# A scheduled attention and Hyena kernel: the order of work behind the first batch laid anew

## The chip, the cores and the metric

One core of one Trainium2 chip runs the whole program. The metric is device time in microseconds (us); the times shown are medians of several runs. A profile is one execution with the hardware profiler on. The engines are PE (matmuls; PEld is its weight load), ACT (activations and copies), DVE (vector work), POOL (casts, and issue of some DMAs) and SP (issues most DMAs).

## The reference

Softmax attention with one added to the denominator (8 batches, 12 heads, 448 positions, 64 wide) gives x, 448 x 768 for a batch. A Hyena-like layer follows: x is projected to three parts, the second is convolved along the sequence with a given filter by FFT, the three are multiplied, and the product is projected again.

```python
attn = e / (np.sum(e, axis=-1, keepdims=True) + np.exp(-m) + 1e-09)
x = np.matmul(attn, v)                # then heads side by side: (B, 448, 768)
proj = x @ w_proj                     # 768 -> 3 * 768
x1, x2, x3 = proj[..., :D], proj[..., D:2*D], proj[..., 2*D:]
X2 = np.fft.rfft(x2, n=S, axis=1)
H = np.fft.rfft(filter_fft, n=S, axis=0)[None, :, :]
y = x1 * np.fft.irfft(X2 * H, n=S, axis=1) * x3
out = y @ w_out
```

## The kernel before

Everything is bf16 on PE with f32 sums in PSUM's eight banks. The work is cut into 2,137 tasks, each some instructions of one engine: `attention(i)` makes them for each of 48 pairs of heads (scores L871 and L873, exponentials L884 and L890 on ACT, products with v L902 and L910, division L923 to L925 on DVE), `staged(b)` and `loaded(b)` make the loads of q, k and v on SP and their casts on POOL, and `dense(b)` makes, for each batch, the folding (L1055, L1060), the second part's projection (L1083 or L1105), the short transforms (L1154, L1158, back L1253), the gates (L1206, L1222) and the last projection (L1019), copied out by ACT (L1332) and stored by SP (L1339, L1342).

A `Plan` collects the tasks. `add` gives each the next number of the table `plan.ORDER`; `run` then lets each engine take its tasks strictly by that number, and a model of the engines and DMAs decides which PSUM bank each task gets. `plan.TIMES` holds durations and lateness of DMAs for that model. The model also says where PE would stand idle between 4.6 and 44 us; `fillers` puts matmuls of zeros there (`fill`, L1501), each 128 columns, as many as fit in nine tenths of the modelled gap. Every engine runs its own queue in order; between engines there are semaphores.

The softmax is computed without taking the maximum off. `watch()` checks that this was safe: the smallest denominator is reduced on DVE (`judge`, L1417, L1418), a one-column matmul counts the bad rows (L1424), and DVE casts the count to the integer `flag` (L1426). Behind all planned tasks each engine loads `flag` into a register (L1559) and branches on it (L1561): if it isn't zero, everything is computed again in a safe form; with this input the branch is jumped over. The last projections of the last batch (five groups of six matmuls, with eight copies and six stores) are kept back and run behind that branch by `plan.rest()`. A hint ahead of the plan names the branch for PE and DVE alone.

```python
add("DVE", 0.35, tau(NHP * n_batches, 4.0), judge, need=[("low", b) for b in range(n_batches)], make=["bad"])
add("PE", 0.1, tau(NHP * n_batches, 4.0), lambda: nc.tensor.matmul(bank(hy)[0:1, 0:1], bad, one), need=["bad"],
    make=["count bad"], take=[hy])
add("DVE", 0.1, tau(NHP * n_batches, 4.0), lambda: nc.vector.tensor_copy(flag, bank(hy)[0:1, 0:1]), need=["count bad"],
    make=["flag"], give=[hy])
...
tc.mark_branch_hint_location("overflow", 0, engines=[E.PE, E.DVE])
plan.run()
...
overflow = nc.values_load(flag[0:1, 0:1], min_val=0, max_val=128)
with (
    tc.If(overflow > 0, label="overflow"),
```

Of the kernel before, what the change touches and what calls it, by code (L numbers as in the profile page):

```python
# [317 lines left out]
def kernel(  # L318
# [104 lines left out]
    def stage(g, at, n):  # L423
# [4 lines left out]
    plan = Plan(  # L428
        {
            "e": 6, "er": 2, "e3": 3, "er3": 1, "k0": 2, "q0": 2, "u": 1, "w": 1, "xf": 1,  # L430
            "x2": 1, "x2s": 1, "x2b": 2, "xs": 2, "t0": 2, "t1": 2, "yh": 1, "g": 1, "x1": 2, "cr": 2, "cw": 1, "cv": 2, "yT": 1, "yR": 1,
            "os": 3,
        }
    )
# [1125 lines left out]
    with (  # L1560
# [6 lines left out]
        for b in range(n_batches):  # L1567
            W["yT", b], W["yR", b // 2] = y, yr
            stable(b)
            plan = Plan(plan.size)  # L1570
# [9 lines left out]
    with tc.manual_schedule(engines={E.PE, E.Pool, E.DVE, E.Activation, E.SP}):  # L1580
        plan = main
# [31 lines left out]
```

## Time and profile before

| what | us |
|---|---|
| median of 3 runs | 369.39 |
| lowest and highest run | 368.69, 369.54 |
| the profiled execution's own time | 367.79 |
| its span, first to last instruction | 366.0 |

The profile's page lists the busy time of each engine, the costliest groups of instructions by source line, and the DMA queues. Other views of the same trace list waits (who waited for whom), the instructions in order of time with runs of like ones merged, all instructions of one line, and the chain of work that ended last. The DMA queue of the loads is at work 72.5% of the span, and 43.86 MB are read from HBM. In a view, "PEldq", "ACTq" or "SPq" is an engine's sequencer, which loads registers, branches and issues DMAs.

### The profile page before, as it was taken

How to read it: one execution, taken by the hardware profiler on the slowest of the kernel's cores; microseconds unless marked ns; L12 is line 12 of the kernel's file. 1: busy time of each engine (PE TensorE's matmuls, PEld its weight loads, DVE VectorE, ACT ScalarE, POOL GpSimd, SP SyncE). 2: the span in 40 equal slices, each digit the busy share in tenths (PEclk: the TensorE clock that was granted, in tenths of full speed). 3: DMA queues.
4: the chain of work that ended last, by engine and by line, in shares of the span. 5: the costliest groups of instructions: out<-in, count | busy, mean ns of one | idle time of the engine just before them, and what ended most of it. 6: DMA issues, size and time to landing. Idle time of an engine off the chain costs nothing. (4 is left out here: it accounts for less than half of the span.)

```text
span 366.0 us, 9373 instructions
## 1 busy us (share of the span) xinstructions
PE 359.8 (98%) x3625; PEld 216.4 (59%) x3625; DVE 259.1 (71%) x672; ACT 264.0 (72%) x454; POOL 115.9 (32%) x247
## 2 busy tenths in 40 slices
PE   8999999999999999999999999999999999999995
PEld 7666676666664766555465555655555556555553
DVE  5669398975889667574887667694478857758670
ACT  6998778777778688767678566778877884464443
POOL 8773482253443463413516343521110000000000
PEclk9999999999999999999999999999999999999999
DMA  8999999998999969899999999864964155044035
GB/s 215 279 246 245 238 180 228 246 190 199 193 256 281 214 204 217 226 226 183 264 226 240 270 211 238 246 162 108 204 119 130 45 88 131 0 88 131 1 134 175
DMA packets 132163, 68.41 MB, mean 187 GB/s; under 512 B 88781, under 2 KB 128528, under 8 KB 132112
## 3 DMA queue, kind: packets, MB, share of 16 engines
q1 hardware_dynamic: 127392, 62.11, 72.5%
q0 software_dynamic: 4480, 5.41, 8.6%
q8 instruction: 29, 0.48, 0.6%
q10 hardware_dynamic: 240, 0.23, 0.3%
q14 instruction: 22, 0.18, 0.1%
HBM read 43.86 MB, written 11.01 MB: 150 GB/s over the span
## 5 line engine op out<-in xcount | busy, mean ns | idle before, releaser
L884 ACT ACTIVATE e<-psum 128x896 bf16<-128x896 f32 x138 | 121.9, 920 | 25.6 <-PE psum L871 22.5
L1206 PE MATMUL psum<-xT,wproj_bf 128*128 128x448 bf16 x576 | 121.9, 353 | 0.0
L1206 PEld LDWEIGHTS <-wproj_bf 128*128 128x128 bf16 x576 | 54.2, 98 | 48.1 <-issue 3.9
L1019 PE MATMUL psum<-wout_bf,yT 128*128 128x384 bf16 (+2 forms) x288 | 54.9, 326 | 0.1
L910 PE MATMUL psum<-vn,e 128*128 128x65 bf16 x1104 | 44.8, 194 | 0.0
L910 PEld LDWEIGHTS <-e 128*128 128x128 bf16 x1104 | 39.4, 98 | 7.5 <-issue 3.6
L871 PE MATMUL psum<-qT,kT 64*128 64x448 bf16 x288 | 42.8, 354 | 0.1
L668 POOL CAST nat<-nat 112x512 bf16<-112x512 f32 x36 | 24.9, 695 | 53.4 <-DMA nat<-in_q_dram 53.3
L1332 ACT COPY osb<-psum 128x384 f32<-128x384 f32 (+2 forms) x56 | 26.0, 482 | 20.3 <-PE psum L1019 15.4
L1172 DVE TENSOR_TENSOR t<-xs,hrs 112x768 bf16<-112x768 bf16 (+1 forms) x64 | 36.5, 589 | 3.8 <-ACT xs L1166 3.4
L1019 PEld LDWEIGHTS <-yT 128*128 128x128 bf16 x288 | 26.7, 98 | 18.3 <-issue 1.4
L1105 PE MATMUL psum<-xf,wproj_bf 128*128 128x456 bf16 x180 | 37.5, 356 | 0.0
L1166 ACT CAST xs<-psum 112x384 bf16<-112x384 f32 (+1 forms) x64 | 28.9, 487 | 11.8 <-PE psum L1154 9.2
L1222 DVE TENSOR_TENSOR g<-x,psum 128x448 bf16<-128x448 bf16 x42 | 25.8, 617 | 14.2 <-PE psum L1206 9.6
L925 DVE TENSOR_TENSOR xb<-psum,den 128x512 bf16<-128x512 f32 x48 | 33.2, 691 | 1.6
L700 POOL CAST vn<-nat 128x192 bf16<-128x192 f32 x58 | 22.6, 421 | 33.5 <-DMA nat<-in_v_dram 33.4
L1220 ACT CAST x<-psum 128x448 bf16<-128x448 f32 x42 | 22.2, 538 | 13.7 <-PE psum L1206 13.4
L1262 ACT CAST cr<-psum 128x452 bf16<-128x452 f32 x48 | 24.1, 543 | 8.4 <-PE psum L1253 8.2
L890 ACT ACTIVATE er<-psum 128x448 bf16<-128x448 f32 x46 | 25.3, 553 | 6.5 <-PE psum L873 5.3
L688 POOL CAST nat<-nat 128x384 bf16<-128x384 f32 x29 | 17.0, 587 | 33.3 <-DMA nat<-in_k_dram 25.1
L923 DVE TENSOR_SCALAR den<-psum 128x8 f32<-128x8 f32 x48 | 7.8, 163 | 27.7 <-PE psum L910 19.7
L1105 PEld LDWEIGHTS <-wproj_bf 128*128 128x128 bf16 x180 | 16.8, 98 | 16.7 <-issue 1.9
(138 smaller groups left out, 499.9 us busy)
## 6 DMA issues: line engine op xcount, KB each, us to landing
nat<-in_q_dram SPq DMA_DIRECT2D x47, 224.0 KB, 4.4
out_dram<-osb SPq DMA_DIRECT2D x23, 384.0 KB, 3.6
nat<-in_k_dram SPq DMA_DIRECT2D x41, 192.0 KB, 4.1
nat<-in_v_dram SPq DMA_DIRECT2D x41, 192.0 KB, 4.7
wproj_bf<-in_moe_w_proj_dram POOLq DMA_DIRECT2D x2, 1152.0 KB, 12.1
rests<-in_k_dram SPq DMA_DIRECT2D x8, 192.0 KB, 5.2
rests<-in_v_dram SPq DMA_DIRECT2D x8, 192.0 KB, 4.2
out_dram<-osb SPq DMA_DIRECT2D x8, 192.0 KB, 2.9
```

The source lines that it names most:

```text
L871: nc.tensor.matmul(sc[:, u, 0:S], kT[b % 2][c, hp, t, :], qT[b % 2][c, hp, :])
L884: nc.scalar.activation(to, of, AF.Exp, scale=SCALE)
L890: nc.scalar.activation(to, of, AF.Exp, scale=SCALE)
L910: nc.tensor.matmul(out_bank(u)[:, n, :], P["e"][1 + t][:, u * S + n * 128 : u * S + n * 128 + 128], vn[b % 2][:, hp, 4 * u + t, :], start= ...
L925: nc.vector.tensor_tensor(W["xb", b][:, hp].rearrange("p n (u d) -> p u n d", u=2), op[:, :, :, 0:DH], rec[:].unsqueeze(3).to_broadcast([1 ...
L1019: nc.tensor.matmul(ops[:n, : c.stop - c.start], y[:, dt, 0:n], wout_bf[:, dt, c], start=(dt == 0), stop=(dt == NDT - 1),)
L1105: nc.tensor.matmul(pps, wproj_bf[:, kt, D + dt * 128 : D + (dt + 1) * 128], W["xf", b][:, kt], start=(kt == 0), stop=(kt == NDT - 1),)
L1166: nc.scalar.copy(L["xs", par, ch][:K, pg % 2, :], L["Z", pg, ch][:K, :DCH])
L1172: nc.vector.tensor_tensor(t[:K], L["xs", par, ch][:K], h, op=ALU.mult)
L1206: nc.tensor.matmul(p[:, :S], wproj_bf[:, kt, 2 * part * D + dt * 128 : 2 * part * D + (dt + 1) * 128], xT()[:, kt, 0:S], start=(kt == 0), ...
L1222: nc.vector.tensor_tensor(g[:, dt, :], L["x1", dt], p[:, :S], op=ALU.mult)
L1332: (nc.vector.tensor_copy if half else nc.scalar.copy)(L["os", st][:n, c.start + lo : c.start + hi], L["O", st, ch][:n, lo:hi])
```

## The change

Two tables of numbers are replaced, and nothing else. `plan.ORDER` has 2,137 numbers as before, of which 1,484 differ. `plan.TIMES` has other values of DMA lateness for 56 early loads (mostly some tenths of a microsecond more). Both lines are cut here to the start of the first table, its last four numbers, and one changed entry of the second.

```diff
-    plan.ORDER = (3, 0, 1, 159, 1, 2, 0, 0, 1,
...
-    4, 488, 666, 498)
-    plan.TIMES = {
...
-    36: (0.58, 0.735, 50.0, -0.6553),
...
+    plan.ORDER = (3, 0, 1, 166, 1, 2, 0, 0, 1,
...
+    4, 466, 707, 547)
+    plan.TIMES = {
...
+    36: (0.58, 0.735, 50.0, -0.0382),
...
```

The last three numbers of ORDER are those of `judge` on DVE, of the counting matmul on PE and of the flag's cast on DVE: in the change the matmul is PE's 708th task of 714 instead of its 667th, and the cast is DVE's 548th task of 549 instead of its 499th, the last one ahead of the branch.

On PE the first 138 tasks stand as before. Behind them 488 tasks have another place, by up to some forty places. The other queues are laid anew from about the same stage on: of DVE's 549 tasks 399 have another place, of ACT's 452 320, of SP's 244 172, of POOL's 178 105.

The flag on PE. The place in the last batch's short transforms where the counting product stood before (`ft` is the transform's table, `x_5282` the second part of the last batch, `bad` and `one` the check's operands):

```order
L1105 LDWEIGHTS wproj_bf
L1105 MATMUL psum<-xf,wproj_bf 128x456
L1154 LDWEIGHTS ft
L1154 MATMUL psum<-x_5282,ft 113x384
L1424 LDWEIGHTS bad
L1424 MATMUL psum<-one,bad 1x1
L1154 LDWEIGHTS ft
L1154 MATMUL psum<-x_5282,ft 113x384
L1206 LDWEIGHTS wproj_bf
L1206 MATMUL psum<-xT,wproj_bf 128x448
```

and the end of PE's planned work in the change (`yR` and `yT` are the gated product, `wout_bf` the last projection's weights):

```order
L1019 LDWEIGHTS yR
L1019 MATMUL psum<-wout_bf,yR 128x384
L1424 LDWEIGHTS bad
L1424 MATMUL psum<-one,bad 1x1
L1019 LDWEIGHTS yT
L1019 MATMUL psum<-wout_bf,yT 128x384
L1019 LDWEIGHTS yT
L1019 MATMUL psum<-wout_bf,yT 128x384
L1559 TENSOR_LOAD flag
L1561 COMPARE_AND_BRANCH
```

The product moved from amid the last batch to two matmuls ahead of the branch. In the change the end of DVE's planned work reads

```order
L1222 TENSOR_TENSOR g<-x_5651,psum 128x448
L1282 TENSOR_TENSOR cv<-cw 128x2x224
L1297 TENSOR_TENSOR yR<-g,cv 128x2x64
L1297 TENSOR_TENSOR yT<-g,cv 128x768
L1426 CAST flag<-psum 1x1
L1559 TENSOR_LOAD flag
L1561 COMPARE_AND_BRANCH
```

so that nothing stands between the cast of the flag and the loads of it. On SP the load of the flag stood ahead of three stores of the last planned rows,

```order
L1339 DMA out_dram<-osb 128x768 x2
L1559 TENSOR_LOAD flag
L1559 ISA x2
L1339 DMA out_dram<-osb 128x768 x3
L1561 COMPARE_AND_BRANCH
```

and in the change it stands behind all of them, directly ahead of the branch:

```order
L1122 DMA_TRANSPOSE x_5301<-nat 128x12x128
L1342 DMA out_dram<-osb 64x768 x2
L1339 DMA out_dram<-osb 128x768 x4
L1559 TENSOR_LOAD flag
L1561 COMPARE_AND_BRANCH
```

The idle matmuls of the first stage. With the new lateness the model sees longer gaps at two places of the part whose order is kept: six matmuls of zeros ahead of the first product with v of the first pair of heads (L902), where there were none, and nineteen instead of nine ahead of the fifth pair's transposition (L562). The first place, a piece of PE's difference, of whose six added pairs of rows the first is shown:

```order
 L871 LDWEIGHTS kT_89
 L871 MATMUL psum<-qT_91,kT_89 128x448
+L1501 LDWEIGHTS idle
+L1501 MATMUL psum<-idle 128x128
...
 L902 LDWEIGHTS er_102
 L902 MATMUL psum<-vn_93,er_102 128x65
```

Sixteen such matmuls are added in all.

More of the change, by code (lines that the diff above doesn't have):

```diff
@@ new lines @@
+    plan.TIMES = {3: (0.64, 0.05, 256.0, 0.0), 15: (0.58, 0.735, 50.0, 0.104), 16: (0.58, 1.17, 50.0, -0.215), 18: (0.52, 0.773, 50.0, 0.499), 20: (0.58, 0.735, 50.0, 0.744), 21: (0.58, 1.17, 50.0, 0.279), 32: (0.58, 0.735, 50.0, 0.639), 34: (0.58, 0.944, 50.0, 0.516), 36: (0.58, 0.735, 50.0, -0.0382), 41: (0.58, 0.735, 50.0, 0.453), 43: (0.58, 0.944, 50.0, 0.574), 45: (0.58, 0.735, 50.0, 0.1294), 50: (0.58, 0.735, 50.0, 0.233), 52: (0.58, 0.944, 50.0, 0.69), 54: (0.58, 0.735, 50.0, 0.0455), 59: (0.58, 0.735, 50.0, -0.3314), 61: (0.58, 0.944, 50.0, 0.2506), 63: (0.58, 0.735, 50.0, -1.4834), 68: (0.58, 0.735, 50.0, 0.1275), 70: (0.58, 0.944, 50.0, -0.1693), 72: (0.58, 0.735, 50.0, 1.6103), 77: (0.58, 0.735, 50.0, 2.7374), 78: (0.58, 1.17, 50.0, -1.7316), 80: (0.58, 0.944, 50.0, -0.5645), 82: (0.58, 0.735, 50.0, -0.0455), 83: (0.58, 1.17, 50.0, 0.0515), 91: (0.58, 0.735, 50.0, 4.0603), 93: (0.58, 0.944, 50.0, 2.4621), 95: (0.58, 0.735, 50.0, 1.4687), 100: (0.58, 0.735, 50.0, -0.854), 102: (0.58, 0.944, 50.0, 3.8075), 104: (0.58, 0.735, 50.0, 3.1933), 109: (0.58, 0.735, 50.0, -0.0054), 111: (0.58, 0.944, 50.0, 1.7322), 113: (0.58, 0.735, 50.0, 0.1213), 118: (0.58, 0.735, 50.0, -0.769), 120: (0.58, 0.944, 50.0, 4.6255), 122: (0.58, 0.735, 50.0, -2.5531), 127: (0.58, 0.735, 50.0, -0.766), 129: (0.58, 0.944, 50.0, 0.8276), 131: (0.58, 0.735, 50.0, -0.6237), 136: (0.58, 1.17, 50.0, 0.5123), 137: (0.58, 1.17, 50.0, 0.15), 141: (0.58, 0.944, 50.0, 3.2579), 143: (1.29, 0.65, 0.2, 1.1461), 144: (0.58, 0.735, 50.0, 3.8397), 146: (1.29, 0.6, 0.2, -0.39), 147: (0.58, 0.735, 50.0, 0.15), 149: (0.58, 0.944, 50.0, 3.7157), 151: (1.29, 0.65, 0.2, -0.415), 152: (0.58, 0.735, 50.0, 3.5606), 154: (1.29, 0.6, 0.2, 0.9439), 155: (0.58, 0.735, 50.0, 0.15), 157: (0.58, 0.944, 50.0, 0.8821), 159: (1.29, 0.65, 0.2, -0.415), 160: (0.58, 0.735, 50.0, 0.6141), 162: (1.29, 0.6, 0.2, -0.39), 163: (0.58, 0.735, 50.0, 0.15), 165: (0.58, 0.944, 50.0, 0.15), 167: (1.29, 0.65, 0.2, -0.415), 168: (0.58, 0.735, 50.0, 0.15), 170: (1.29, 0.6, 0.2, -0.39), 171: (0.58, 0.735, 50.0, 2.7438), 173: (0.58, 0.944, 50.0, 0.15), 175: (1.29, 0.65, 0.2, -0.415), 176: (0.58, 0.735, 50.0, 0.15), 178: (1.29, 0.6, 0.2, -0.39), 179: (0.58, 0.735, 50.0, 0.15), 181: (0.58, 0.944, 50.0, 0.15), 183: (1.29, 0.65, 0.2, -0.415), 184: (0.58, 0.735, 50.0, 0.15), 186: (1.29, 0.6, 0.2, -0.39), 187: (0.58, 0.735, 50.0, 0.15), 189: (0.58, 1.17, 50.0, 0.15), 190: (0.58, 1.17, 50.0, 0.15), 194: (0.58, 0.944, 50.0, 0.15), 196: (1.53, 1.55, 0.2, -0.363), 197: (0.58, 0.735, 50.0, 0.15), 199: (1.53, 1.65, 0.2, -0.214), 200: (0.58, 0.735, 50.0, 0.15), 202: (0.58, 0.944, 50.0, 0.15), 204: (0.58, 0.735, 50.0, 0.15), 206: (0.58, 0.735, 50.0, 0.15), 208: (0.58, 0.944, 50.0, 0.15), 210: (0.58, 0.735, 50.0, 0.15), 212: (0.58, 0.735, 50.0, 0.15), 214: (0.58, 0.944, 50.0, 0.15), 216: (1.53, 1.55, 0.2, -0.363), 217: (0.58, 0.735, 50.0, 0.15), 219: (1.53, 1.65, 0.2, -0.214), 220: (0.58, 0.735, 50.0, 0.15), 222: (0.58, 0.944, 50.0, 0.15), 224: (0.58, 0.735, 50.0, 0.15), 226: (0.58, 0.735, 50.0, 0.15), 228: (0.58, 0.944, 50.0, 0.15), 230: (0.58, 0.735, 50.0, 0.15), 232: (0.58, 0.735, 50.0, 0.15), 234: (0.58, 1.17, 50.0, 0.15), 235: (0.58, 1.17, 50.0, 0.15), 239: (0.58, 0.944, 50.0, 0.15), 241: (1.53, 1.55, 0.2, -0.363), 242: (0.58, 0.735, 50.0, 0.15), 244: (1.53, 1.65, 0.2, -0.214), 245: (0.58, 0.735, 50.0, 0.15), 247: (0.58, 0.944, 50.0, 0.15), 249: (0.58, 0.735, 50.0, 0.15), 251: (0.58, 0.735, 50.0, 0.15), 253: (0.58, 0.944, 50.0, 0.15), 255: (0.58, 0.735, 50.0, 0.15), 257: (0.58, 0.735, 50.0, 0.15), 259: (0.58, 0.944, 50.0, 0.15), 261: (1.53, 1.55, 0.2, -0.363), 262: (0.58, 0.735, 50.0, 0.15), 264: (1.53, 1.65, 0.2, -0.214), 265: (0.58, 0.735, 50.0, 0.15), 267: (0.58, 0.944, 50.0, 0.15), 269: (0.58, 0.735, 50.0, 0.15), 271: (0.58, 0.735, 50.0, 0.15), 273: (0.58, 0.944, 50.0, 0.15), 275: (0.58, 0.735, 50.0, 0.15), 277: (0.58, 0.735, 50.0, 0.15), 279: (0.58, 1.17, 50.0, 0.15), 280: (0.58, 1.17, 50.0, 0.15), 284: (0.58, 0.944, 50.0, 0.15), 286: (1.53, 1.55, 0.2, -0.363), 287: (0.58, 0.735, 50.0, 0.15), 289: (1.53, 1.65, 0.2, -0.214), 290: (0.58, 0.735, 50.0, 0.15), 292: (0.58, 0.944, 50.0, 0.15), 294: (0.58, 0.735, 50.0, 0.15), 296: (0.58, 0.735, 50.0, 0.15), 298: (0.58, 0.944, 50.0, 0.15), 300: (0.58, 0.735, 50.0, 0.15), 302: (0.58, 0.735, 50.0, 0.15), 304: (0.58, 0.944, 50.0, 0.15), 306: (1.53, 1.55, 0.2, -0.363), 307: (0.58, 0.735, 50.0, 0.15), 309: (1.53, 1.65, 0.2, -0.214), 310: (0.58, 0.735, 50.0, 0.15), 312: (0.58, 0.944, 50.0, 0.15), 314: (0.58, 0.735, 50.0, 0.15), 316: (0.58, 0.735, 50.0, 0.15), 318: (0.58, 0.944, 50.0, 0.15), 320: (0.58, 0.735, 50.0, 0.15), 322: (0.58, 0.735, 50.0, 0.15), 324: (0.58, 1.17, 50.0, 0.15), 325: (0.58, 1.17, 50.0, 0.15), 329: (0.58, 0.944, 50.0, 0.15), 331: (1.53, 1.55, 0.2, -0.363), 332: (0.58, 0.735, 50.0, 0.15), 334: (1.53, 1.65, 0.2, -0.214), 335: (0.58, 0.735, 50.0, 0.15), 337: (0.58, 0.944, 50.0, 0.15), 339: (0.58, 0.735, 50.0, 0.15), 341: (0.58, 0.735, 50.0, 0.15), 343: (0.58, 0.944, 50.0, 0.15), 345: (0.58, 0.735, 50.0, 0.15), 347: (0.58, 0.735, 50.0, 0.15), 349: (0.58, 0.944, 50.0, 0.15), 351: (1.53, 1.55, 0.2, -0.363), 352: (0.58, 0.735, 50.0, 0.15), 354: (1.53, 1.65, 0.2, -0.214), 355: (0.58, 0.735, 50.0, 0.15), 357: (0.58, 0.944, 50.0, 0.15), 359: (0.58, 0.735, 50.0, 0.15), 361: (0.58, 0.735, 50.0, 0.15), 363: (0.58, 0.944, 50.0, 0.15), 365: (0.58, 0.735, 50.0, 0.15), 367: (0.58, 0.735, 50.0, 0.15), 369: (0.58, 1.17, 50.0, 0.15), 370: (0.58, 1.17, 50.0, 0.15), 374: (0.58, 0.944, 50.0, 0.15), 376: (1.53, 1.55, 0.2, -0.363), 377: (0.58, 0.735, 50.0, 0.15), 379: (1.53, 1.65, 0.2, -0.214), 380: (0.58, 0.735, 50.0, 0.15), 382: (0.58, 0.944, 50.0, 0.15), 384: (0.58, 0.735, 50.0, 0.15), 386: (0.58, 0.735, 50.0, 0.15), 388: (0.58, 0.944, 50.0, 0.15), 390: (0.58, 0.735, 50.0, 0.15), 392: (0.58, 0.735, 50.0, 0.15), 394: (0.58, 0.944, 50.0, 0.15), 396: (1.53, 1.55, 0.2, -0.363), 397: (0.58, 0.735, 50.0, 0.15), 399: (1.53, 1.65, 0.2, -0.214), 400: (0.58, 0.735, 50.0, 0.15), 402: (0.58, 0.944, 50.0, 0.15), 404: (0.58, 0.735, 50.0, 0.15), 406: (0.58, 0.735, 50.0, 0.15), 408: (0.58, 0.944, 50.0, 0.15), 410: (0.58, 0.735, 50.0, 0.15), 412: (0.58, 0.735, 50.0, 0.15), 415: (0.82, 1.584, 40.0, -1.0544), 416: (0.82, 1.584, 40.0, 1.208), 417: (1.79, 4.157, 37.0, -4.3366), 418: (0.82, 4.751, 116.0, -2.7673), 419: (0.82, 4.751, 116.0, 0.8831), 420: (0.82, 5.866, 100.0, 1.4863), 565: (1.53, 1.6, 0.2, -0.155), 603: (1.53, 1.6, 0.2, -0.155), 640: (1.53, 1.6, 0.2, -0.155), 678: (1.53, 1.6, 0.2, -0.155), 715: (1.53, 1.6, 0.2, -0.155), 753: (1.53, 1.6, 0.2, -0.155), 790: (1.53, 1.6, 0.2, -0.155), 828: (1.53, 1.6, 0.2, -0.155), 865: (1.53, 1.6, 0.2, -0.155), 903: (1.53, 1.6, 0.2, -0.155), 940: (1.53, 1.6, 0.2, -0.155), 978: (1.53, 1.6, 0.2, -0.155), 1015: (1.53, 1.6, 0.2, -0.155), 1054: (1.53, 1.6, 0.2, -0.155), 1185: (0.62, 1.172, 50.0, -0.626), 1191: (0.62, 1.172, 50.0, -0.626), 1196: (0.62, 1.172, 50.0, -0.626), 1317: (0.62, 1.172, 50.0, -0.626), 1323: (0.62, 1.172, 50.0, -0.626), 1328: (0.62, 1.172, 50.0, -0.626), 1333: (1.35, 1.533, 180.0, 0.034), 1454: (0.62, 1.172, 50.0, -0.626), 1460: (0.62, 1.172, 50.0, -0.626), 1465: (0.62, 1.172, 50.0, -0.626), 1484: (1.6, 1.5, 0.2, -0.208), 1495: (1.6, 1.5, 0.2, -0.208), 1584: (0.62, 1.172, 50.0, -0.626), 1590: (0.62, 1.172, 50.0, -0.626), 1595: (0.62, 1.172, 50.0, -0.626), 1600: (1.35, 1.533, 180.0, 0.034), 1619: (1.6, 1.5, 0.2, -0.208), 1630: (1.6, 1.5, 0.2, -0.208), 1719: (0.62, 1.172, 50.0, -0.626), 1725: (0.62, 1.172, 50.0, -0.626), 1730: (0.62, 1.172, 50.0, -0.626), 1749: (1.6, 1.5, 0.2, -0.208), 1756: (1.6, 1.5, 0.2, -0.208), 1849: (0.62, 1.172, 50.0, -0.626), 1855: (0.62, 1.172, 50.0, -0.626), 1860: (0.62, 1.172, 50.0, -0.626), 1865: (1.35, 1.533, 180.0, 0.034), 1884: (1.6, 1.5, 0.2, -0.208), 1891: (1.6, 1.5, 0.2, -0.208), 1984: (0.62, 1.172, 50.0, -0.626), 1990: (0.62, 1.172, 50.0, -0.626), 1995: (0.62, 1.172, 50.0, -0.626), 2014: (1.6, 1.5, 0.2, -0.208), 2021: (1.6, 1.5, 0.2, -0.208), 2114: (1.35, 1.533, 180.0, 0.034), 2120: (0.62, 1.172, 50.0, -0.626), 2125: (0.62, 1.172, 50.0, -0.626), 2128: (0.45, 0.6, 50.0, -0.45), 2132: (0.45, 0.6, 50.0, -0.45)}
```

3 lines of the change are left out of this document (1 added, 2 removed).

## The prediction

> **What bounds the kernel now.** I read the page's busy table first.
>
> ```profile
> PE 359.8 (98%) x3625; PEld 216.4 (59%) x3625; DVE 259.1 (71%) x672; ACT 264.0 (72%) x454; POOL 115.9 (32%) x247
> ...
> PEclk9999999999999999999999999999999999999999
> ```
>
> PE, the matrix engine, is busy 98% of the 366.0 us and its granted clock is full in every slice, while the next engine stands at 72%. But matmuls overlap, so a busy PE may still be slow. Two more views settle that: what PE waited for, and how far apart its matmuls start.
>
> ```profile
> PE psum L1509 <- DVE idle L1497: 1.1, 1, 1.1
> PE psum L823 <- DVE xT L995: 0.4, 1, 0.4
> PE psum L873 <- DVE qT L592: 0.2, 1, 0.2
> PE psum L596 <- POOL ks L551: 0.2, 1, 0.2
> ```
>
> ```profile
> L1206 PE MATMUL psum<-xT,wproj_bf 128*128 128x448 bf16 x576 | 121.9, 353 | 0.0
> ```
>
> ```profile
> 100.41 2.44 PE L1206 MATMUL psum<-xT,wproj_bf 128*128 128x448 bf16 x12
> 30.87 0.32 PE L823 MATMUL psum<-uw,ft 113*112 113x384 bf16 x1 [0.43 <-DVE xT L995]
> ```
>
> The waits table (total us, times, longest) holds four waits, 1.9 us together, the latest of them at 30.87 us. Twelve 448-column matmuls take 2.44 us; with the last one's own 0.353 taken off, that is 11 steps of 0.19 us, and the mean duration over all 576 is the same 353 ns as here, so this stretch is typical. From 31 us on, then, the profile shows one unbroken stream of matmuls: **the time is the stream plus the two ends**. The last piece is read from the chain that ended last and the stores:
>
> ```profile
> 357.20 2.12 PE psum L1019 x12
> ...
> 359.86 2.48 DMA out_dram<-osb
> ```
>
> The matmuls kept for behind the branch begin at 357.20, and the stores end the span.
>
> All terms below are for the profiled execution: 367.79 us, its span of 366.0 and 1.8 around it. The median of the timed runs, 369.39, stands 1.6 above it; I add the terms to the median.
>
> **Term 1, the flag at the end.** The flag's path and the branch, each engine's own register load of the flag (L1559) and its branch (L1561; EVENT_SEMAPHORE is the first thing run behind it). Durations in ns, then the start:
>
> ```profile
> L1424 PE MATMUL psum<-one,bad x1: 164/164/164, 329.7 to 329.7; 128*1 128x1 bf16 x1
> L1426 DVE CAST flag<-psum x1: 140/140/140, 331.6 to 331.6; 1x1 int32<-1x1 f32 x1
> L1559 SPq TENSOR_LOAD <-flag x1: 860/860/860, 333.1 to 333.1; - x1
> L1559 ACTq TENSOR_LOAD <-flag x1: 955/955/955, 351.9 to 351.9; - x1
> L1559 PEldq TENSOR_LOAD <-flag x1: 484/484/484, 355.7 to 355.7; - x1
> ```
>
> ```profile
> L1561 SPq EVENT_SEMAPHORE  x8: 17/17/17, 355.5 to 356.0; - x8
> L1561 SPq COMPARE_BRANCH  x1: 58/58/58, 351.6 to 351.6; - x1
> L1561 ACTq COMPARE_BRANCH  x1: 50/50/50, 352.9 to 352.9; - x1
> L1561 ACTq EVENT_SEMAPHORE  x1: 17/17/17, 355.9 to 355.9; - x1
> L1561 PEldq COMPARE_BRANCH  x1: 393/393/393, 356.3 to 356.3; - x1
> ```
>
> ```profile
> 356.56 1.61 PE L1019 MATMUL psum<-wout_bf,yT 128*128 128x384 bf16 x7
> 357.23 1.63 ACT L1332 COPY osb<-psum 128x384 f32<-128x384 f32 x4 [4.36 <-PEq L1561]
> 350.26 1.32 SPq L1339 DMA_DIRECT2D out_dram<-osb  x3
> 358.11 1.15 SPq L1342 DMA_DIRECT2D out_dram<-osb  x2
> 359.86 3.43 SPq L1339 DMA_DIRECT2D out_dram<-osb  x4
> 361.67 0.59 ACT L1332 COPY osb<-psum 128x512 f32<-128x512 f32 x1 [0.86 <-PE psum L1019]
> ```
>
> Before, the flag was written at 331.6, so every engine loaded it when it liked: SP at 333.1, ACT at 351.9, and what follows their branches (2.95 us from the end of ACT's branch to its next instruction, 3.85 on SP) passed beside PE's stream and was over at 355.5 to 355.9, before the first kept matmul. In the change the flag's product stands two matmuls before the branch, and the flag's cast is DVE's last instruction. On the old clock those two matmuls start at 356.56; the product takes 0.16 there, the cast 0.14, two handovers some 0.05 each (an estimate): the flag is there at **356.95**. Behind it:
> - PE: from the start of its load, 355.7, to the first kept matmul, 357.20, it took 1.5. Now 356.95 + 1.5 = 358.45: **+1.2**.
> - ACT: 356.95 + 0.96 + 0.05 + 0.05 between = 358.0, + 2.95 = 360.95, + 0.5 for the string of semaphore waits ahead of its first copy (SP's eight take that long) = 361.45. Its copies then follow each other at (1.63 - 0.48)/3 = 0.38: the 512-wide one, seventh, starts at 363.75 instead of 361.67: +2.1 there, of which the wait for PE that it had before gives part back; the end of ACT's copies is about **+1.7**.
> - SP: 356.95 + 0.86 + 0.06 + 0.1 between = 357.95, + 3.85 = 361.8, + 0.6 for the eight semaphores = 362.4. The six store issues that were spread out by waiting for data now stand back to back: 1.15 for two, 0.08 between, 0.44 for each further one (1.32/3). The sixth starts at 362.4 + 1.15 + 0.08 + 3 x 0.44 = 364.95; before, at 359.86 + 3.43 - 0.33 = 362.96. **+2.0**.
>
> These run beside each other, so the largest counts: SP's +2.0. The last data are there for it: ACT ends at 362.93 + 1.7 = 364.6.
>
> [...]
>
> **Term 2, sixteen more idle matmuls ahead of the moved part.** They are fixed work on PE:
>
> ```profile
> 12.53 0.36 PE L871 MATMUL psum<-qT,kT 64*128 64x448 bf16 x2
> 12.72 0.28 PE L902 MATMUL psum<-vn,er 64*128 64x65 bf16 x8
> ...
> 13.92 0.35 PE L873 MATMUL psum<-qT,kT 128*128 128x448 bf16 x1
> 14.21 0.86 PE L871 MATMUL psum<-qT,kT 64*128 64x448 bf16 x4
> ...
> 17.24 0.67 PE L1501 MATMUL psum<-idle 128*128 128x128 bf16 x9
> 17.75 0.22 PE L562 MATMUL psum<-ident_bf,ks 128*128 128x128 bf16 x1
> 18.03 0.34 PE L564 MATMUL psum<-ident_bf,ldm 128*128 128x128 bf16 x3
> ```
>
> One costs (0.67 - 0.22)/8 = 0.056. Six go between 12.53 and 12.72, where PE did not wait (0.19 is the plain step), and they put a 128-row matmul between 64-row ones: such a change of rows costs 0.29 (13.92 to 14.21) less 0.19, so 0.10, twice. 6 x 0.056 + 0.20 = 0.54. Ten go to the nine at 17.24: nineteen end at 18.30, the next starts at 18.36 instead of 18.03: 0.33. Together 0.87. Cover: four matmuls in two pairs at 14.21 should take 0.36 + 0.19 but took 0.86, a wait of 0.3, and the 0.43 at 30.87. **I take 0.2**, the 0.87 less this cover, rounded up; ends 0 (loads later than in the profiled execution make the gaps real) and 1.1 (16 x 0.056 + 0.20, nothing hidden).
>
> **Term 3, the moved work itself.** From PE's first moved matmul (L1253, about 64 us) on, the same matmuls stand in another order; counted in the two orders the changes of row count differ only by the two above. A PE without a wait after 31 us leaves nothing to win in this execution: the gain's end is 0. SP's loads and POOL's casts are moved too. Their room:
>
> ```profile
> POOL nat L668 <- DMA nat<-in_q_dram: 53.3, 14, 12.7
> ```
>
> POOL stands idle up to 12.7 us for a load and is at work a third of the time, so a cast that moves by a few places stays hidden. The loss has no row. The nearest is a matmul group that is set one place too early and waits for what that place was to cover: 6 x 0.19 = 1.1. **I take 0**, ends 0 and 2.3 (two such).
>
> Sum: 2.0 + 0.2 + 0 = 2.2. The profiled execution would take 370.0; **369.39 + 2.2 = 371.6 us**.
>
> **Rivals.**
> - *A, a new wait in the stream.* One or two groups too early, 1.1 to 2.3 on top: 372.7 to 373.9. For it: 1,484 of 2,137 numbers of the order differ, and the old stream had no wait left to lose. Against: ACT and DVE at 72% have room.
> [...]
> - *C, on the other side: late loads.* The timed runs lie 0.9 to 1.75 us above the profiled one. If that is PE waiting for loads that come late after 64 us, an order with more room between SP's loads and their users saves up to that: 371.6 - 1.6 = 370.0, not slower. [...] For it: the spread. Against: the profile shows no such wait, and the stretch before 64 us, where loads are tightest, keeps its order.
>
> **How the numbers follow.** 0.3% (1.1 us) is about what a measurement of this kernel can tell from no change: 368.28 to 370.50 counts as the same. Forecast 0.50, its own range 370.6 (PE's +1.2 alone) to 372.6. A 0.20, all slower. B 0.12: same 0.09, faster 0.03 (with C). C 0.18: same 0.13, faster 0.05. So slower 0.70, same 0.22, faster 0.08. The range leaves out the gains at the bottom and A's upper half at the top: 369.0 to 373.4.
>
> **What would show it.** Right: in the profile of the changed kernel ACT and SP load the flag only when DVE has cast it, at about 357 us; they resume 3 to 4 us after their branches; the first kept matmul comes about 1.5 us after PE's load; the last store issue starts about 2 us later against PE's last matmul ahead of the branch. Term 2 is right if the transpositions at 18.03 start late and the wait at 30.87 is gone. Term 3 is right if the waits table shows none for PE after 31 us. Wrong: a kept matmul about 0.5 us behind PE's load with ACT and SP ready (B); PE waits of about a microsecond in the middle (A); a median below 370.5 with term 1 in full (C).

## The result, and the profile after

| | before | after |
|---|---|---|
| median, us | 369.47 (4 runs, 368.69 to 370.02) | 374.54 (4 runs, 373.97 to 375.54) |
| ratio | | 1.014, 95% interval 1.0114 to 1.0166 |
| profiled execution and its span, us | 367.79, 366.0 | 375.03, 373.2 |

The change costs 5.1 us. The forecast was 371.6, 2.2 us more, with a range up to 373.4: the sign was right, the size less than half. The page of the changed kernel, its busy times and PE's granted clock in 40 slices:

```profile
PE 360.7 (97%) x3640; PEld 216.1 (58%) x3641; DVE 260.8 (70%) x672; ACT 263.1 (70%) x454; POOL 112.9 (30%) x247
...
PEclk9999999999999999999999999999999999999998
```

PE's busy time has grown by only 0.9 us while the span grew by 7.2, so PE stands still somewhere; and in the last slice its granted clock is under nine tenths of full speed (the digit 8), where every slice of before has a 9. The waits table of the changed kernel (total us, times, longest) says where it stands:

```profile
PE psum L1019 <- ACTq L1561: 3.8, 1, 3.8
PE psum L871 <- DMA kT<-nat: 2.5, 1, 2.5
PE psum L1509 <- DVE idle L1497: 1.1, 1, 1.1
PE psum L596 <- POOL ks L551: 1.0, 1, 1.0
...
```

The first row is new: PE's first kept matmul waits 3.8 us for what **ACT's** sequencer does at the branch's line. The second (at 73.5 us) and the fourth are waits for loads and casts of the early stages, longer in this execution than in the one of before, which had no wait for kT at all; what they are worth is left to the experiments. The flag's path, by the views of single lines:

```profile
L1426 DVE CAST flag<-psum x1: 146/146/146, 358.8 to 358.8; 1x1 int32<-1x1 f32 x1
...
L1559 ACTq TENSOR_LOAD <-flag x1: 462/462/462, 359.0 to 359.0; - x1
...
L1559 PEldq TENSOR_LOAD <-flag x1: 489/489/489, 359.0 to 359.0; - x1
```

```profile
L1561 SPq EVENT_SEMAPHORE  x8: 17/17/17, 363.2 to 363.7; - x8
L1561 ACTq COMPARE_BRANCH  x1: 50/50/50, 359.5 to 359.5; - x1
L1561 SPq COMPARE_BRANCH  x1: 54/54/54, 359.6 to 359.6; - x1
...
L1561 PEldq COMPARE_BRANCH  x1: 388/388/388, 359.6 to 359.6; - x1
...
L1561 PEldq EVENT_SEMAPHORE  x1: 51/51/51, 360.1 to 360.1; - x1
...
L1561 ACTq EVENT_SEMAPHORE  x1: 17/17/17, 362.9 to 362.9; - x1
...
  PE psum L1019: 3.8, 1
```

All engines load the flag at 359.0, the instant DVE has cast it, and branch at 359.5 to 359.6. PE's own sequencer is through at 360.1. ACT's first instruction behind the branch comes at 362.9, SP's at 363.2, some 3.4 and 3.6 us behind their branches. The last row, of the list of who waited for this line, names PE. Its matmuls in order of time, and the granted clock of three stretches (length, PE busy, clock, DMA share, GB/s):

```profile
358.73 0.50 PE L1019 MATMUL psum<-wout_bf,yT 128*128 128x384 bf16 x2
363.00 4.21 PE L1019 MATMUL psum<-wout_bf,yT 128*128 128x384 bf16 x16 [3.77 <-ACTq L1561]
```

```profile
358.00:363.00 5.00, 1.23 (x8) 0.96 0.04 10
363.00:366.00 3.00, 3.00 (x10) 0.50 0.08 20
366.00:369.60 3.60, 3.44 (x21) 1.00 0.85 281
```

Sixteen matmuls took 4.21 us; before, twelve took 2.12, about 0.16 from start to start. The middle stretch shows why: from 363 to 366 the clock is half, 0.50, and in the single records the starts lie 0.32 apart. ACT's copies and SP's stores behind the branch:

```profile
363.82 1.77 ACT L1332 COPY osb<-psum 128x384 f32<-128x384 f32 x4 [8.29 <-SPq L1561]
```

```profile
364.71 1.12 SPq L1342 DMA_DIRECT2D out_dram<-osb  x2
367.11 3.43 SPq L1339 DMA_DIRECT2D out_dram<-osb  x4
```

ACT, ready at 362.9, waits with its first copy for what **SP** does at the branch's line, which ends at 363.7. The last four store issues take 3.43 us, as long as before.

**Where the 5.1 us lie.** The last planned matmul starts at 358.90 and the first kept one at 363.00: 4.10 apart, 0.47 in the trace of before, so +3.63. From start to start, eight steps of 0.32 and one on either side of them (0.27 and 0.24), where before has 0.16, add 1.45. Together 5.08. Measured over the whole tail, from the start of the last two planned matmuls to the span's end, before took 9.44 and after takes 14.47: +5.03. The medians differ by 5.07. So the loss lies in the last 15 us; the other 2.2 us between the two profiled spans lie ahead of them, where this execution has the longer waits for loads.

### The profile page after: what moved, and what is told of

Read it like the earlier page. It is cut to its first block, busy times and chain, and to the rows that moved or that the text cites. A ratio compares the mean times of both kernels' runs of the same rounds, so it can differ in the third digit from the quotient of the medians.

```text
span 373.2 us, 9396 instructions
## 1 busy us (share of the span) xinstructions
PE 360.7 (97%) x3640; PEld 216.1 (58%) x3641; DVE 260.8 (70%) x672; ACT 263.1 (70%) x454; POOL 112.9 (30%) x247
## 5 line engine op out<-in xcount | busy, mean ns | idle before, releaser
L1206 PEld LDWEIGHTS <-wproj_bf 128*128 128x128 bf16 x576 | 53.6, 98 | 47.5 <-issue 4.5
L1019 PE MATMUL psum<-wout_bf,yT 128*128 128x384 bf16 (+2 forms) x287 | 56.0, 332 | 3.8 <-ACTq L1561 3.8
L910 PEld LDWEIGHTS <-e 128*128 128x128 bf16 x1104 | 40.4, 98 | 6.9 <-issue 2.0
L668 POOL CAST nat<-nat 112x512 bf16<-112x512 f32 x36 | 23.5, 656 | 54.0 <-DMA nat<-in_q_dram 53.8
L1172 DVE TENSOR_TENSOR t<-xs,hrs 113x768 bf16<-113x768 bf16 (+1 forms) x64 | 36.9, 594 | 3.6 <-ACT xs L1166 3.5
L1105 PE MATMUL psum<-xf,wproj_bf 128*128 128x456 bf16 x180 | 38.5, 356 | 0.0
L1166 ACT CAST xs<-psum 113x384 bf16<-113x384 f32 (+1 forms) x64 | 28.8, 487 | 10.4 <-PE psum L1154 7.9
L700 POOL CAST vn<-nat 128x192 bf16<-128x192 f32 x58 | 21.6, 400 | 40.9 <-DMA nat<-in_v_dram 27.4
L688 POOL CAST nat<-nat 128x384 bf16<-128x384 f32 x29 | 16.0, 554 | 37.6 <-DMA nat<-in_k_dram 35.6
L1083 PE MATMUL psum<-wproj_bf,xf 128*113 128x384 bf16 x144 | 26.4, 328 | 0.0
```

The source lines that it names most:

```text
L910: nc.tensor.matmul(out_bank(u)[:, n, :], P["e"][1 + t][:, u * S + n * 128 : u * S + n * 128 + 128], vn[b % 2][:, hp, 4 * u + t, :], start= ...
L1019: nc.tensor.matmul(ops[:n, : c.stop - c.start], y[:, dt, 0:n], wout_bf[:, dt, c], start=(dt == 0), stop=(dt == NDT - 1),)
L1083: nc.tensor.matmul(pps[:FQ, :DCH], W["xf", b][:, kt, pg, 0:FQ], wproj_bf[:, kt, D + ch * DCH : D + (ch + 1) * DCH], start=(kt == 0), stop= ...
L1105: nc.tensor.matmul(pps, wproj_bf[:, kt, D + dt * 128 : D + (dt + 1) * 128], W["xf", b][:, kt], start=(kt == 0), stop=(kt == NDT - 1),)
L1166: nc.scalar.copy(L["xs", par, ch][:K, pg % 2, :], L["Z", pg, ch][:K, :DCH])
L1172: nc.vector.tensor_tensor(t[:K], L["xs", par, ch][:K], h, op=ALU.mult)
```

## Experiments

The theory, T: the flag's late place is the whole loss, and all other moved work is worth nothing. Its parts: F, what makes the late flag dear is the time that an engine without the branch hint needs behind its branch (ACT's 3.4 and SP's 3.6 us above); K, PE's stand of 3.77 us lowers its clock (to the 0.50 above). The rivals: the moved order or the added idle matmuls cost something of their own; loads come late (L).

| run | what it is | ratio to before, 95% | median, us |
|---|---|---|---|
| e0_before | before once more | | 369.76 (one run) |
| e1_flag_early | after, flag's tasks at their old places | 1.0006, 0.9983 to 1.0030 | 369.34 |
| e2_flag_late | before, flag's tasks at the new places | 1.0114, 1.0075 to 1.0153 | 373.58 |
| e3_hints | after, branch hint for ACT and SP too | 1.0041, 1.0013 to 1.0070 | 370.75 |
| e9_hint_act | after, hint for ACT, not SP | 1.0136, 1.0085 to 1.0188 | 374.61 |
| e10_hint_sp | after, hint for SP, not ACT | 1.0142, 1.0069 to 1.0214 | 374.66 |
| e5_warm | after, PE kept busy while it waits | 1.0103, 1.0072 to 1.0134 | 373.23 |
| e4_hints_before | before, hint for ACT and SP too | 1.0001, 0.9983 to 1.0018 | 368.79 |
| e6_early_hints | e1 with the hints of e3 | 1.0025, 1.0006 to 1.0044 | 370.04 |
| e7_fillers | before with after's lateness table | 0.998, 0.996 to 1.000 | 368.52 |
| e11_fillers_again | the same again | 0.9994, 0.9958 to 1.0030 | 368.46 |
| e8_order_alone | e1 with before's lateness table | 0.9996, 0.9966 to 1.0026 | 369.13 |

Before ran beside them with medians of 368.83 (e1 to e3), 369.01 (e4 to e7) and 369.17 (e8 to e11).

### The flag's place alone, both ways

```diff
 e1_flag_early, the changed kernel's ORDER:
-    4, 466, 707, 547)
+    4, 466, 666, 498)
 e2_flag_late, the ORDER of before:
-    4, 488, 666, 498)
+    4, 488, 707, 547)
```

> The changed order, only the counting product and the flag's cast are put back amid the last batch. Theory T (the flag's place is the whole loss: PE's kept matmuls wait for ACT's restart behind the branch, and then run at half rate): 369.0 to 370.3 us, the first kept matmul less than 0.6 us behind the last planned one, no slow matmuls. Rival S (half of the loss lies in the moved stream, as the wait of 2.5 us for kT in the changed kernel's profile suggests): 371.5 us or more.

> The order of before, only the counting product and the flag's cast are put to the end. Theory T: 374.0 to 375.0 us, PE idle for 3.5 to 4 us behind its last planned matmul, then matmuls of 384 columns 0.32 us apart. Rival S: 371 to 372.5 us, since the stream of before is kept.

With the flag early, 1,482 changed numbers and sixteen more idle matmuls are left, and nothing measurable is lost; the tail, measured as above, takes 9.4 us again. With the flag late in the old order, 1.14% is lost; the median, 373.58, is a little under the 374 to 375 expected. PE's waits in e1:

```profile
PE psum L871 <- DMA kT<-nat: 1.4, 1, 1.4
PE psum L596 <- POOL ks L551: 1.2, 1, 1.2
PE psum L1509 <- DVE idle L1497: 1.1, 1, 1.1
PE psum L1206 <- ACT cr L1262: 0.6, 1, 0.6
...
```

The wait on L1561 is gone; that for kT is there, too, in a kernel that is no slower than before. And e2 in order of time:

```profile
356.72 0.16 PE L1424 MATMUL psum<-one,bad 128*1 128x1 bf16 x1
356.82 0.50 PE L1019 MATMUL psum<-wout_bf,yT 128*128 128x384 bf16 x2
361.27 1.14 PE L1019 MATMUL psum<-wout_bf,yT 128*128 128x384 bf16 x6 [3.96 <-ACTq L1561]
363.01 3.72 PE L1019 MATMUL psum<-wout_bf,yT 128*128 128x384 bf16 x13 [0.61 <-ACT osb L1332]
```

The same stand and, from 363.01, the same slow stretch (clock 0.52 from 363 to 366) appear in the order of before; the first six matmuls behind the stand still run at full rate (1.14 us), and PE then stands once more, for ACT's copy. T holds as far as the intervals tell: the flag's place is the loss, and what e1 leaves room for beside it is 0.3%.

### What PE waits for: the hint, for both engines and for one

```diff
-        tc.mark_branch_hint_location("overflow", 0, engines=[E.PE, E.DVE])
 e3_hints:
+        tc.mark_branch_hint_location("overflow", 0, engines=[E.PE, E.DVE, E.Activation, E.SP])
 e9_hint_act:
+        tc.mark_branch_hint_location("overflow", 0, engines=[E.PE, E.DVE, E.Activation])
 e10_hint_sp:
+        tc.mark_branch_hint_location("overflow", 0, engines=[E.PE, E.DVE, E.SP])
```

> The changed kernel with the branch named ahead for ACT and SP too, not for PE and DVE alone. [...]

> The changed kernel with the hint for the branch given for ACT too, and not for SP. Theory H (PE is held by ACT's restart alone): the first kept matmul comes 1.4 us behind the last planned one instead of 4.1, at full rate. SP then still restarts 3.6 us behind its branch, and my own working for SP becomes testable: its stores would end the span about 2 us later than in before, ratio 1.0055 with the working as on record, against 1.004 if SP's six issues fit in anyway (as with both hints). Rival (SP's restart holds PE as well): the wait of 3.8 us and the half rate stay, ratio 1.014.

> The changed kernel with the hint for SP and not for ACT. Theory H: nothing is won, PE still waits 3.8 us for ACT's restart and runs at half rate behind it, granted clock 0.995; ratio 1.013 to 1.014. If SP's restart is what holds the end, ratio about 1.009.

With both hints, by the branch's line in e3:

```profile
L1561 SPq EVENT_SEMAPHORE  x8: 17/17/17, 362.6 to 363.1; - x8
L1561 ACTq COMPARE_BRANCH  x1: 68/68/68, 362.1 to 362.1; - x1
L1561 SPq COMPARE_BRANCH  x1: 74/74/74, 362.1 to 362.1; - x1
...
L1561 ACTq EVENT_SEMAPHORE  x1: 17/17/17, 362.5 to 362.5; - x1
```

```profile
362.82 2.45 PE L1019 MATMUL psum<-wout_bf,yT 128*128 128x384 bf16 x14 [1.09 <-DVEq L1561]
```

ACT and SP go on 0.4 and 0.5 us behind their branches instead of 3.4 and 3.6, PE's first kept matmul, which now waits for DVE's sequencer, comes 1.42 us behind the last planned one instead of 4.10, and seven tenths of the loss are gone (1.014 to 1.0041). F holds: the time behind the branch goes with the hint. If so, 370.5 to 371.5 us and restarts within 1 us of the branches were expected, otherwise 374 to 375 us; 370.75 was measured. What the 3 us without the hint consist of is not shown. The DMA view of the changed kernel lists five packets of queues that it labels "instruction" between the branches and ACT's restart (all within 360.3 to 361.1, the restart is at 362.9); whose code they hold, and whether an engine waited for them, it doesn't say.

The single hints were to show that ACT alone holds PE. **That part of the theory fell.** With SP hinted and not ACT nothing is won, as foreseen:

```profile
PE psum L1019 <- ACTq L1561: 3.5, 1, 3.5
...
```

But with ACT hinted and not SP nothing is won either. First e9's branch line, then its PE and its ACT:

```profile
L1561 SPq EVENT_SEMAPHORE  x8: 17/17/17, 361.1 to 361.7; - x8
...
L1561 ACTq EVENT_SEMAPHORE  x1: 17/17/17, 358.2 to 358.2; - x1
```

```profile
358.49 1.15 PE L1019 MATMUL psum<-wout_bf,yT 128*128 128x384 bf16 x6 [1.09 <-DVEq L1561]
362.34 4.04 PE L1019 MATMUL psum<-wout_bf,yT 128*128 128x384 bf16 x15 [2.70 <-ACT osb L1332]
```

```profile
361.81 2.18 ACT L1332 COPY osb<-psum 128x384 f32<-128x384 f32 x5 [8.10 <-SPq L1561]
```

ACT is ready at 358.2 and PE runs the first group of six at 358.49, 1.09 behind its last, as in e3. The next group needs the copy of an earlier result out of PSUM, and ACT's first copy at 361.81 waits for **SP's** restart at 361.1. So PE stands 2.70 us one group later, and the half rate follows there, too, from 363.6 on. The three engines form a chain: PE waits for ACT, ACT for SP, and each unhinted one alone costs the whole 5 us (1.0136 in e9, 1.0142 in e10).

### Whether the stand itself lowers the clock

```diff
         plan.run()
+        at = plan.banks["ho", ("O", n_batches - 1, 2, 1)][0]
+        for _ in range(50):
+            nc.tensor.matmul(psum[:, 512 * at : 512 * at + 128], idle, idle)
```

> The changed kernel with 50 idle matmuls (128 columns, written to a PSUM bank that nobody reads) on PE behind the last planned matmul and ahead of PE's load of the flag; nothing else is moved. At 0.056 us each they take about 2.8 us, and they lie within the 3.8 us in which PE waits for ACT's restart. Theory T+K (flag late: PE is held by ACT's restart, and a PE that has stood idle for 3.9 us then runs its first matmuls at half rate): the wait for ACT shrinks to about 1 us and ends at the same place, about 4.2 us behind the last planned matmul; the 384-column matmuls behind it start 0.162 apart from the first instead of 0.32; the tail shrinks by 1.4 us, ratio to the kernel before about 1.010 (373.1). [...]

The idle products fall into the bank of one output piece, so this run leaves that piece's sums out; the kept matmuls, copies and stores are all there.

```profile
359.37 2.96 PE L1560 MATMUL psum<-idle 128*128 128x128 bf16 x50
362.69 1.14 PE L1019 MATMUL psum<-wout_bf,yT 128*128 128x384 bf16 x6 [0.36 <-ACTq L1564]
364.45 1.30 PE L1019 MATMUL psum<-wout_bf,yT 128*128 128x384 bf16 x7 [0.63 <-ACT osb L1332]
```

```profile
363.00:366.00 3.00, 2.37 (x16) 1.00 0.05 13
```

The wait ends 3.48 us behind the last planned matmul, and behind it the clock is 1.00 where the changed kernel had 0.50; six matmuls take 1.14 us again. All runs' clocks agree: the mean over the span was 0.995 in each of the changed kernel's four, 0.997 to 1.00 in these four. PE ends 1.3 us earlier against the flag's product (9.57 us behind it, 10.86 in the changed kernel). K holds: this kernel runs the same code behind the same branch, without the hints, and at full rate, so the half rate came with the stand and not with the branch. The 1.3 us are not the clock's alone, since ACT was back 0.6 us sooner here. Of them the span's end gains 0.7 in the profiled execution, since ACT's copies (0.63 above) and the stores then come late; by the ratios it is 0.4%, though the two intervals overlap.

### The terms that were set near nothing, and single executions

```diff
 e7_fillers and e11_fillers_again, in the kernel before:
-    plan.TIMES = {... 36: (0.58, 0.735, 50.0, -0.6553), ...
+    plan.TIMES = {... 36: (0.58, 0.735, 50.0, -0.0382), ...
 e8_order_alone, in e1_flag_early:
-    plan.TIMES = {... 36: (0.58, 0.735, 50.0, -0.0382), ...
+    plan.TIMES = {... 36: (0.58, 0.735, 50.0, -0.6553), ...
```

> The kernel before with the changed kernel's table of lateness alone (no task is moved): the planner then puts the 16 further idle matmuls ahead of the early attention groups, 6 and 10. My term 2: +0.2 us, ends 0 and 1.1, so ratio 1.0005, at most 1.003. Rival G (they cost their full 0.87 and the moved order wins this back in the changed kernel): ratio 1.0024, first moved work about 0.9 us later.

> The kernel before with the changed kernel's table of lateness alone, a second time, beside the moved order alone: whether its ratio of 0.998 [0.996, 1.000] is a gain. If the further idle matmuls win something (early transpositions that wait less, steadier loads): again 0.997 to 0.999. If they are worth nothing: 0.999 to 1.002.

> The changed kernel's order with the flag's product and cast back at their old places, and with the table of lateness of before, so that the planner puts no further idle matmuls: the moved work alone (my term 3). Term 3 as forecast: ratio 1.000, within 0.998 to 1.002, and the waits table of PE shows nothing after 64 us that before's executions do not show as well. Rival A (the moved order costs a place or two in the stream): 1.003 to 1.006, with waits or steps of 0.3 us and more between 64 and 330 us. Rival C (the new order gives loads more room): ratio below 0.998.

> The kernel before with the hint for the branch given for ACT and SP too. Theory F: ACT's and SP's first instruction behind the branch follow it by about 0.5 us instead of 2.95 and 3.85, but PE reached its first kept matmul without waiting for them anyway: ratio 0.999 to 1.000 (0 to 0.4 us won from ACT's copies standing ready). Rival (the restart was on the end's path before, too): first kept matmul earlier by 0.5 us or more, ratio below 0.998.

> The changed kernel's order with the flag's product and cast back at the places they had before (the work between them moved as in the change), and the hint for the branch given for ACT and SP too. [...] Rival (ACT's and SP's restart still costs something at the end of before, in store issues): ACT's and SP's first instruction behind the branch comes 3 us earlier against PE and the ratio falls below 0.998.

> The kernel of before once more, for a second profile. Theory L (late loads in the part that both orders share make PE wait for kT near 72 us, and the first profile of before happened to be free of it): a wait of PE for kT of 0.5 to 2.5 us between 65 and 75 us, and the time above 367.8 by about that. Rival S (the wait comes from the moved order): no such wait.

The sixteen idle matmuls give 0.998 and 0.9994, so nothing is lost, and the first run's small gain did not show again. The moved order alone gives 0.9996, and its PE waits are few:

```profile
PE psum L1509 <- DVE idle L1497: 1.1, 1, 1.1
PE psum L564 <- POOL ldm L523: 0.7, 1, 0.7
PE psum L1206 <- ACT cr L1262: 0.6, 1, 0.6
...
```

The first two belong to the early stages. The third ends at 332.2 us, behind the place where the flag's product was put back (329.8); e1 and e6 have it, too, the changed kernel (above) has not. So it came with the edit, not with the change, and what is measured here as the moved order's worth holds up to 0.6 us against it.

The hints are worth nothing in before (1.0001) and nothing with the flag early (e6 at 1.0025 is no better than e1 at 1.0006, and a little above the 0.998 to 1.002 that were expected; whether moved order, idle matmuls and hints together cost a tenth or two of a per cent stays open). Single executions of an unmoved order do wait for late loads. Before once more, and below it the unusually long profiled execution of e4 (372.69 us), by PE's waits:

```profile
...
PE psum L564 <- POOL ldm L523: 0.9, 1, 0.9
PE psum L1206 <- DVE g L1222: 0.5, 1, 0.5
PE psum L871 <- DMA kT<-nat: 0.3, 1, 0.3
...
```

```profile
PE psum L564 <- POOL ldm L523: 2.0, 3, 0.9
PE psum L1154 <- DMA x<-xb: 1.2, 1, 1.2
...
```

So executions of both orders wait for late loads, and profiled spans differ by microseconds for it. (e3's traced execution, 373.94 us, lies 3.2 above its median; PE stood 2.6 us for DVE near 50 us in it, at half clock behind that.) But L as it was expected, 0.5 us or more for kT between 65 and 75 us, was not there in e0: 0.3, at 87. Waits for kT of 1.4 to 2.5 us near 73 were seen in three traces of the moved order alone (after, e1, e5), and none in its other five; the old order had 0.5 for kT at most (e2), and 0.7 for qT near 75 (e7). Whether the moved order makes them likelier stays open. In the medians it doesn't show (e1 1.0006, e8 0.9996), so it is no part of the change's 5.1.

## Why the prediction was wrong

- **The failed step is in term 1: "These run beside each other, so the largest counts: SP's +2.0."** They don't. In its place the runs showed a chain: PE's first kept matmul waits for ACT's restart (3.8 us), ACT's copies wait for SP's (the changed kernel and e9), and so the ends that I took the largest of lie one behind the other. PE paid ACT's time, +3.63, instead of its own +1.2. A row that I quoted could have told it: ACT's copy at 357.23 stood with `[4.36 <-PEq L1561]`, an engine waiting for another engine's work at the branch. I read the rows of before only for when each engine was ready, and there ACT (355.9) was ready before PE (357.20), so that PE's wait for it could not be seen.
- **The half rate behind the stand was not thought of at all**: +1.45 of the 5.08. The working held the matmul's 0.16 for fixed, since the clock had shown a 9 in every slice.
- The pieces of term 1 were well sized, but for one. The flag's two handovers, estimated at 0.05 each, took about 0.04 and 0.02 (the product ends at 358.79, the cast runs from 358.83 to 358.98, the loads start at 359.0). ACT was to go on 4.0 us behind the flag (360.95 - 356.95) and does after 3.9 (362.9 - 359.0); SP was to be back 4.85 behind it and is back after 4.2. PE by itself was to lose 1.2; in e3, where only DVE's sequencer holds it, it loses 1.42 - 0.47 = 0.95. That ACT's copies were to start 4.5 behind the flag and start 4.8 behind it is luck: they waited for SP. Wrong was that the six store issues would stand back to back: the last four took 3.43 us as before, since their data came late, too.
- Term 2 (+0.2) and term 3 (0) held within what was measured: e1 1.0006, e7 and e11 0.998 and 0.9994, e8 0.9996. The matmul at 30.87, whose wait of 0.43 was to give cover, comes at 31.05 in the changed kernel, 0.18 later, behind a wait of about 0.25.
- Rival A, a new wait amid the stream, has no price in the runs: e8's interval ends at 1.0026, or 1.0 us, below A's least price of 1.1. The changed kernel's trace did show the wait named as A's sign, the 2.5 us for kT; e1 has 1.4 of it and is no slower. Rival B (0.12 of the chances), by which ACT's and SP's late start is not the branch's, is refuted by e3: its sign, a kept matmul about 0.5 us behind PE's load, was 4.0 in the changed kernel, and ACT and SP go on 3.4 and 3.6 us behind their branches without the hint, 0.4 and 0.5 with it. Rival C, an order that takes late loads better: no gain in e1 or e8.
- Of the signs named ahead for term 1, ACT's and SP's late loads and restarts were there. Two were not: "the first kept matmul comes about 1.5 us after PE's load" was 4.0 (359.0 to 363.0), the very step that failed, and the last store issue came 5.1 us later against PE's last planned matmul, not 2 (it ended 11.64 behind that matmul's start, 6.56 before). Of term 2's, the transpositions came late (18.56 for 18.03), the wait was not gone; term 3's, no wait after 31 us, was not there.

## What to carry to other kernels

Where engines meet at a branch or barrier, draw who waits for whom behind it before adding up late starts: here ACT's start held PE (3.8 us) and SP's held ACT's copies (ready at 362.9, the first at 363.82), and a wait that ended in time before leaves no row to warn of it. A flag for a rare path should be computed as early as its data allow, or the hint given to all engines that go on behind the branch: here it won nothing for ACT or SP alone (1.0136, 1.0142) and seven tenths of the loss for both (1.0041). A stand of PE can cost more than its length: here 3.77 us of it were followed by 3.0 us of matmuls at half rate, 1.45 us on top.

## What was unexpected of the hardware

- Behind the branch without the hint ACT and SP took 3.4 and 3.6 us to their next instruction (ACT 2.8 to 3.6 over e2, e5 and e10), with the hint 0.4 and 0.5 (e3).
- The lowered clock lasted the same time, 3.4 us, in five traces. In the changed kernel 0.96 over 5.0 us makes 0.4 us of half clock (0.04 x 5.0 / 0.5), then 3.0 us at 0.50: 3.4 in all. In e9, where PE stood 2.70 us, by the same view:

```profile
362.30:364.90 2.60, 2.56 (x13) 0.76 0.40 89
364.90:367.50 2.60, 2.38 (x9) 0.58 0.99 347
```

(0.24 + 0.42) x 2.60 / 0.5 is 3.4 again, and so it is in e2 (0.84 over 1.70 us, then 0.52 over 3.00), in e10 (0.59 over 361 to 364, 0.84 over 364 to 367) and in e3, where PE stood 2.6 us near 50 us (0.91 over 50 to 53, 0.52 over 53 to 56). What sets this length no run shows, nor how long a stand must be for it. In e2 the clock was still full right behind a stand of 3.96 us (1.00 over 357.00 to 361.30, and six matmuls in 1.14 us from 361.27). In e9, where PE had stood 2.70 us, the clock fell at about 363.6 (0.24 x 2.60 / 0.5 = 1.25 us ahead of 364.9), 1.3 us after the matmuls had set in again at 362.34. The 2.5 us at 73.5 us of the changed kernel left the clock full (1.00 over 70 to 80).
